# Attention and a Mish layer on one core: a new order for the head of the kernel, and the last tile in two banks

## The chip, the cores and the metric

The kernel runs on one core of a Trainium2 chip. The metric is device time in microseconds (us) of one execution. A core has a matrix engine (TensorE, PE in the profile; PEld is its weight load), VectorE (DVE), ScalarE (ACT), GpSimd (POOL) and SyncE (SP), which work side by side, each through its own instructions in order. They meet through semaphores. Matrix results go to PSUM, eight banks of 128 x 512 fp32; everything else is in SBUF. DMAs are issued here from SP's queue and from ACT's.

## What is computed

x is 2048 x 512 in bf16. It is normalised once, and two branches read the result and are added to x.

```python
xn = layernorm(x)                                   # over 512, eps 1e-5
# A: linear attention, 32 heads of 16
q, k, v = xn @ wqkv                                 # 512 -> 3 x 512
pq, pk  = q @ w_phi, k @ w_phi                      # 16 x 16 for each head
phi     = concat(softmax(p), softmax(-p))           # for q and for k
kv, z   = phi_k^T v, sum over rows of phi_k         # 32 x 16 for each head
o       = (phi_q kv) / (phi_q z + 1e-6)
# B: a layer with Mish
act     = mish(xn @ w1 + b1)                        # 512 -> 1792
out     = x + o @ wo + act @ w2
```

## The kernel before, in words

The 2048 rows are 16 tiles of 128, four to a group. The order of all instructions is written out by hand: each engine executes what the program text gives it, in that order (`manual_schedule`), and only semaphores and the reuse of buffers make it wait.

w_phi is multiplied into the weights first. `fold` (L93) takes a transposed weight `wT` (512 x 512, read by a DMA transposition on SP, L90) and the block-diagonal `Wbd` (made by DVE at L458), and writes `wkp` for the keys, later `wqp` for the queries. Then `logits(s, i, copy)` (L188) is four matmuls of 128 x 512 and a copy into `p_sb`; s = 0 to 3 are the keys of the four groups, s = 4 to 7 the queries. `value` (L160) is the same with `wv`, copied into `vext`. `hidden(n)` (L168) does n units of the Mish layer, each four matmuls and one Mish on ACT; there are 56 units, 14 to a group.

For a softmax of p and of -p, `extremes(s)` (L194, DVE) subtracts the maximum and the minimum of each 16 columns, `exponentials(s)` (L223, ACT) takes two activations of 128 x 2048, and `normalise(s, k)` (L240, DVE) sums, inverts and multiplies. `accumulate(g)` (L274) adds phi_k^T v into `pkv`, which has three PSUM banks; `mask_kv` (L288) takes it out. For the queries, `attend(h, i)` (L312) multiplies with kv into `pnd` (the same three banks) and four ACT copies take that out; `combine(h)` (L341, DVE) divides and has the result turned by a DMA. `second_layer(t)` (L388) is 14 matmuls for tile t, `project_out(h)` (L397) adds o @ wo for two tiles in the same bank, and `residual` (L409, DVE) adds x and sends the rows out.

**PSUM.** Five banks (`ps`, tag mm) go round among folds, turns, logits, values, hidden units and second-layer tiles: the sixth user waits until the first user's bank has been read. Three banks (`ps2`, tag kv) hold pkv, then pnd; before, they are pkv's from the start, zeroed by DVE at L439.

**The head.** SP issues x's tiles 0 and 1 (L415), the transposition of the keys' weight (L418), then the rest of x, wv, w1. ACT's queue issues w_phi, x's tiles 2 and 3, and b1. Twelve matmuls on the identity (L450) warm PE. `ln_stats` (L110) makes mean and variance of tiles on DVE, and POOL makes the reciprocal root by an add and a power (L119, L122); `ln_apply` (L125) is one DVE instruction for each tile. Tiles 0 to 3 are turned by PE (`ln_turn_pe`, L136), later ones by DMA (`ln_turn_dma`, L144). Then follow fold, logits of group 0, `extremes(0)` with the normalisation of group 1 inside, four values and four hidden units.

**The loop** (L496) has, for s = 0 to 3: exponentials(s), accumulate(s - 1), two values copied by DVE, logits(s + 1), two values copied by ACT, statistics of a later group, normalise(s), hidden units (16, 14, 8, 10), extremes(s + 1). So on ACT the copies of logits(s + 1) come after exponentials(s), and on DVE the value copies come after extremes(s). After the loop come accumulate(3), logits(5), second_layer(0), two hidden units, attend(0, 0), two more, attend(0, 1), second_layer(1), and then a pipeline over eight pairs of tiles (L543). At its end tile 15 has its four matmuls of o @ wo in two halves of 256 columns in one bank, so that the first half can leave while the second is made; DVE reads the bank between them.

## Time and profile before

| | |
|---|---|
| median of 3 runs | 186.38 us (186.23 to 186.47) |
| profiled execution | 186.27 us |
| its span, first to last instruction | 184.5 us |
| mean granted clock of TensorE | 0.996 |
| busy: PE, DVE, ACT, POOL | 175.5, 149.4, 126.8, 8.2 us |
| first real matmul | 6.74 us |
| end of PE's last matmul | 181.4 us |

Times in the views are us from the start of the span. A timeline line has start, duration, engine, line, operation, what it writes <- what it reads, shape, and in brackets the engine's idle time ahead of it with what ended it; like instructions in a row are merged (x4), and the duration then spans all of them. A line of the waits has engine, instruction and line, what it waited for, and the total, the number of times and the longest wait in us. Ends of matmuls are modelled: a matmul of 128 x 512 is shown as 379 ns, but the next one starts 216 ns after it.

### The profile page before, as it was taken

What the parts mean: (1) busy time and instruction counts of PE and PEld (TensorE: products, weight loads), DVE (VectorE), ACT (ScalarE), POOL (GpSimd) and SP (SyncE); (2) the same over time, 40 slices, a digit from 0 to 9 for tenths busy, and PEclk for the clock granted to TensorE, in tenths of its full rate; (3) what the DMA queues carried; (4) which work ended last, traced back from release to release, by engine and by line L of the source; (5) the groups of instructions that cost most, each with busy time, mean ns of one, the idle gap of its engine ahead of it and who ended that gap; (6) DMA issues with size and microseconds to landing.
All of it is one profiled execution on the core that took longest, in us unless ns stands there. A gap on an engine that the chain in (4) does not pass through costs nothing.

```text
span 184.5 us, 2715 instructions
## 1 busy us (share of the span) xinstructions
PE 175.5 (95%) x1011; PEld 89.0 (48%) x1025; DVE 149.4 (81%) x263; ACT 126.8 (69%) x196; POOL 8.2 (4%) x22
## 2 busy tenths in 40 slices
PE   6799879999999999999999999999999999999991
PEld 2454334464444645644464555555554545455440
DVE  4989999987999989989999784299916996738962
ACT  2357999989888799969986999272842567244200
POOL 4403020000200000000000000000000000000000
PEclk9999999999999999999999999999999999999998
DMA  5997899000091000000000922943079302990732
GB/s 144 298 407 240 175 361 205 0 0 5 6 187 35 4 0 0 0 0 4 0 0 1 191 39 56 187 101 60 0 171 207 77 5 58 199 197 2 89 111 88
DMA packets 44394, 18.02 MB, mean 98 GB/s; under 512 B 36829, under 2 KB 43869, under 8 KB 44381
## 3 DMA queue, kind: packets, MB, share of 16 engines
q1 hardware_dynamic: 43408, 17.50, 39.9%
q10 hardware_dynamic: 972, 0.35, 0.7%
q8 instruction: 8, 0.13, 0.3%
q14 instruction: 6, 0.04, 0.1%
HBM read 6.84 MB, written 2.10 MB: 48 GB/s over the span
## 4 chain that ended last, share of the span: by engine, by line
PE 87%; ACT 5%; DVE 3%; DMA 2%; issue 1%
PE po L392 26%; PE ph L174 24%; PE pproj L154 21%; PE po L403 7%; PE pnd L323 4%; PE pkv L279 4%; ACT e L226 2%; DMA x_sb<-in_A_x_dram 2%; DVE stats L116 1%; ACT acts L181 1%; DVE x_sb L411 1%; ACT L181 1%; ACT L226 0%; PE pfold L98 0%; PE ptr L139 0%
## 5 line engine op out<-in xcount | busy, mean ns | idle before, releaser
L174 PE MATMUL ph<-xnT,w_sb 128*128 128x512 bf16 x224 | 49.7, 379 | 1.2 <-ACT p_sb L192 1.2
L392 PE MATMUL po<-w_sb,acts 128*128 128x512 bf16 x218 | 50.0, 379 | 0.3
L181 ACT ACTIVATE acts<-ph,b1f 128x512 bf16<-128x512 f32 x56 | 35.4, 695 | 3.5 <-PE ph L174 3.2
L174 PEld LDWEIGHTS <-w_sb 128*128 128x128 bf16 x224 | 21.8, 98 | 27.3 <-issue 1.5
L226 ACT ACTIVATE e<-e 128x2048 bf16<-128x2048 bf16 x16 | 29.7, 1902 | 7.2 <-DVE e L216 7.2
L392 PEld LDWEIGHTS <-acts 128*128 128x128 bf16 x224 | 21.5, 98 | 23.3
L154 PEld LDWEIGHTS <-xnT 128*128 128x128 bf16 x192 | 18.3, 97 | 22.6 <-DMA xnT<-xn 1.2
L192 ACT CAST p_sb<-pproj 128x512 bf16<-128x512 f32 x29 | 15.7, 585 | 9.0 <-PE pproj L154 9.0
L411 DVE TENSOR_TENSOR x_sb<-po,x_sb 128x512 bf16<-128x512 f32 (+1 forms) x17 | 10.7, 655 | 13.3 <-PE po L403 13.3
L244 DVE TENSOR_REDUCE s<-e 128x128 f32<-128x2048 bf16 x8 | 18.2, 2279 | 1.6 <-ACT e L226 1.6
L403 PE MATMUL po<-wqk,ob 128*128 128x512 bf16 (+1 forms) x66 | 14.7, 366 | 0.7 <-DVE x_sb L411 0.7
L154 PE MATMUL pproj<-wkp,xnT 128*128 128x512 bf16 x62 | 14.5, 379 | 0.9 <-DMA xnT<-xn 0.8
L154 PE MATMUL pproj<-wv,xnT 128*128 128x512 bf16 x61 | 15.0, 379 | 0.2
L154 PE MATMUL pproj<-wqk,xnT 128*128 128x512 bf16 x63 | 14.4, 379 | 0.1
L332 ACT CAST wkp<-pnd 128x768 bf16<-128x768 f32 x8 | 6.4, 804 | 10.5 <-PE pnd L323 6.5
L205 DVE TENSOR_TENSOR m<-m 128x512 bf16<-128x512 bf16 (+1 forms) x32 | 11.5, 359 | 1.1
L205 DVE TENSOR_TENSOR m<-p_sb 128x1024 bf16<-128x1024 bf16 x16 | 11.0, 685 | 1.0 <-ACT p_sb L192 1.0
L332 ACT CAST wv<-pnd 128x768 bf16<-128x768 f32 x8 | 6.3, 793 | 7.3 <-PE pnd L323 5.1
L323 PEld LDWEIGHTS <-qT 128*128 128x128 bf16 x128 | 9.1, 98 | 3.8
L116 DVE BATCH_NORM_STATS2 stats<-x_sb 128x6 f32<-128x512 bf16 x16 | 9.9, 679 | 1.2 <-DMA x_sb<-in_A_x_dram 1.2
L323 PE MATMUL pnd<-kvm,qT 128*128 128x144 bf16 x128 | 10.6, 226 | 0.1
L403 PEld LDWEIGHTS <-ob 128*128 128x128 bf16 x68 | 6.6, 98 | 7.7 <-issue 0.9
(64 smaller groups left out, 171.2 us busy)
## 6 DMA issues: line engine op xcount, KB each, us to landing
w_sb<-in_B_w_dram SPq DMA_DIRECT2D x2, 1792.0 KB, 8.7
out_dram<-x_sb SPq DMA_DIRECT2D x15, 128.0 KB, 1.8
x_sb<-in_A_x_dram SPq DMA_DIRECT2D x1, 1024.0 KB, 11.2
x_sb<-in_A_x_dram SPq DMA_DIRECT2D x1, 512.0 KB, 4.0
wv<-in_A_wqkv_dram SPq DMA_DIRECT2D x1, 512.0 KB, 4.9
wqk<-in_A_wo_dram SPq DMA_DIRECT2D x1, 512.0 KB
x_sb<-in_A_x_dram SPq DMA_DIRECT2D x1, 256.0 KB, 3.2
x_sb<-in_A_x_dram ACTq DMA_DIRECT2D x1, 256.0 KB, 3.5
```

The costliest lines, as they stand in the source:

```text
L154: nc.tensor.matmul(pp[:], lhsT=xnT[:, t, kt, :], rhs=w[:, kt, :], start=(kt == 0), stop=(kt == KT - 1),)
L174: nc.tensor.matmul(ph[:], lhsT=w1_sb[:, kt, f * P : (f + 1) * P], rhs=xnT[:, g * TPG : (g + 1) * TPG, kt, :], start=(kt == 0), stop=(kt == ...
L181: nc.scalar.activation(acts[:, f, g * 512 : (g + 1) * 512], ph[:], ACT.Mish, bias=b1f[:, f : f + 1])
L192: copy(p_of[s][:, i, :], pp[:])
L205: nc.vector.tensor_tensor(out=m[:], in0=src[:, :, 0:half], in1=src[:, :, half : 2 * half], op=op)
L226: nc.scalar.activation(v, v, ACT.Exp)
L244: nc.vector.reduce_sum(t[:], v.rearrange("p t l (c e) -> p (t l c) e", e=16), axis=AX.X)
L323: nc.tensor.matmul(blocks(pnd, pl, j, 144), lhsT=qT_of[h][:, i, pl * 4 + j, :], rhs=kvm[:, pl, j, :], start=True, stop=True,)
L332: nc.scalar.copy(to[:, :, 0:3, :], a)
L392: nc.tensor.matmul(po[:], lhsT=acts[:, f, t * P : (t + 1) * P], rhs=w2_sb[:, f, :], start=(f == 0), stop=(t == NT - 1 and f == FT - 1),)
L403: nc.tensor.matmul(po[:, c], lhsT=oT_of[h][:, i * 4 + j, :], rhs=wo_sb[:, j, c], start=False, stop=(j == 3 or len(cuts) == 2), skip_group_ ...
L411: nc.vector.tensor_tensor(out=y, in0=po[:, c], in1=y, op=ALU.add)
```

## The change

- ACT's queue issues x's tiles 0 and 1 first, then w_phi, tiles 2 and 3, and wv; SP issues the weight's transposition first, then tiles 4 to 7, b1, w1 and the rest.
- For tiles 0 to 3, the reciprocal root is a Sqrt on ACT (with an eps tile as bias) and a reciprocal on DVE. One Sqrt on eps comes early, behind ACT's DMA issues. Statistics, roots and applications go tile by tile for tiles 0 and 1.
- POOL makes eps first, and takes over the three casts for the masks from DVE. Nine warm-up matmuls instead of twelve.
- PE turns tile 0 before the fold; three of the fold's four blocks go to kv's banks. value(0) comes behind the fold and the turn of tile 1, ahead of the logits.
- Six hidden units instead of four ahead of exponentials(0). In s = 0, the first tile of logits(1) has an ordinary bank and is copied between the two exponentials; the other three go to kv's banks, and one ACT copy of 128 x 1536 takes them out after six further hidden units.
- pkv takes kv's banks after that copy; DVE zeroes it there, between normalise(0, 1) and extremes(1).
- Hidden units: 6, then 6 + 11, 14, 8, 9 and 2, where there were 4, then 16, 14, 8, 10 and 2 + 2. The first eight matmuls of second_layer(1) stand where the last two units stood.
- Tile 15 has two banks: its second layer is made in halves of 256 columns, and so is its o @ wo.

```diff
--- before.py
+++ after.py
@@ -75,6 +75,8 @@
     wqp = wqk[:, :, 0:D]
     wo_sb = wqk[:, :, D : 2 * D]
     ident = consts.tile([P, P], BF16, name="ident")
+    eps = consts.tile([P, 1], FP32, name="eps")
+    root = consts.tile([P, 1], FP32, name="root")
     mhalf = consts.tile([P, TPG], FP32, name="mhalf")
     block = consts.tile([P, 8, 16], BF16, name="block")
     KVmask = consts.tile([P, 136], FP32, name="KVmask")
@@ -90,10 +92,13 @@
         nc.sync.dma_start_transpose(out=wT[:], in_=A_wqkv[:, base_col : base_col + D])
         return wT
 
-    def fold(wT, dst, dve):
+    def fold(wT, dst, dve, banks=None):
 
         for kt in range(KT):
-            pf = ps.tile([P, 512], FP32, name="pfold", tag="mm")
+            if banks is not None and kt < 3:
+                pf = banks[:, kt, :]
+            else:
+                pf = ps.tile([P, 512], FP32, name="pfold", tag="mm")[:]
             for j in range(4):
                 nc.tensor.matmul(
                     pf[:, j * P : (j + 1) * P],
@@ -103,9 +108,9 @@
                     stop=True,
                 )
             if kt in dve:
-                nc.vector.tensor_copy(dst[:, kt, :], pf[:])
+                nc.vector.tensor_copy(dst[:, kt, :], pf)
             else:
-                nc.scalar.copy(dst[:, kt, :], pf[:])
+                nc.scalar.copy(dst[:, kt, :], pf)
 
     def ln_stats(t0, n):
 
@@ -147,12 +152,13 @@
             in_=xn[:, i : i + 2, :].rearrange("p t c -> p (t c)"),
         )
 
-    def project(w, t):
-
-        pp = ps.tile([P, 512], FP32, name="pproj", tag="mm")
+    def project(w, t, pp=None):
+
+        if pp is None:
+            pp = ps.tile([P, 512], FP32, name="pproj", tag="mm")[:]
         for kt in range(KT):
             nc.tensor.matmul(
-                pp[:], lhsT=xnT[:, t, kt, :], rhs=w[:, kt, :],
+                pp, lhsT=xnT[:, t, kt, :], rhs=w[:, kt, :],
                 start=(kt == 0), stop=(kt == KT - 1),
             )
         return pp
@@ -160,7 +166,7 @@
     def value(t, copy):
         pv = project(wv, t)
         copy(
-            vext[(t // TPG) % 2][:, t % TPG, :, 0:128], pv[:].rearrange("p (j c) -> p j c", j=4)
+            vext[(t // TPG) % 2][:, t % TPG, :, 0:128], pv.rearrange("p (j c) -> p j c", j=4)
         )
 
     units = iter([(g, f) for g in range(NG) for f in range(FT)])
@@ -189,7 +195,7 @@
         if i == 0:
             p_of[s] = smx.tile([P, TPG, 512], BF16, name="p_sb", bufs=1)
         pp = project(wkp if s < NG else wqp, (s % NG) * TPG + i)
-        copy(p_of[s][:, i, :], pp[:])
+        copy(p_of[s][:, i, :], pp)
 
     def extremes(s, between=None):
 
@@ -220,8 +226,8 @@
                 op=ALU.subtract,
             )
 
-    def exponentials(s):
-        for k in range(2):
+    def exponentials(s, ks=(0, 1)):
+        for k in ks:
             v = e_of[s][:, 2 * k : 2 * k + 2, :, :]
             nc.scalar.activation(v, v, ACT.Exp)
             if s >= NG:
@@ -268,10 +274,10 @@
         v = kv[:, :, 0:432].rearrange("p b (k c) -> p b k c", c=144)
         return v[:, 0:2, :, c0:c1], v[:, 2, 0:2, c0:c1]
 
-
-    pkv = ps2.tile([P, 3, 512], FP32, name="pkv", tag="kv")
+    kv_of = {}
 
     def accumulate(g):
+        pkv = kv_of[0]
         e = e_of.pop(g)
         for j in range(4):
             for pl in range(2):
@@ -286,7 +292,7 @@
                     )
 
     def mask_kv():
-
+        pkv = kv_of[0]
 
         a, b = by_parts(pkv, 0, 136)
         nc.vector.tensor_tensor(
@@ -385,26 +391,28 @@
                 in_=o_t[:, q].rearrange("p i c -> p (i c)"),
             )
 
-    def second_layer(t):
-        po = ps.tile([P, 512], FP32, name="po", tag="mm")
-        po_of[t] = po
-        for f in range(FT):
-            nc.tensor.matmul(
-                po[:], lhsT=acts[:, f, t * P : (t + 1) * P], rhs=w2_sb[:, f, :],
-                start=(f == 0), stop=(t == NT - 1 and f == FT - 1),
-            )
+    def halves(t):
+        return (slice(0, 256), slice(256, 512)) if t == NT - 1 else (slice(0, 512),)
+
+    def second_layer(t, f0=0, f1=FT):
+        if f0 == 0:
+            po_of[t] = [ps.tile([P, 512], FP32, name="po", tag="mm") for _ in halves(t)]
+        for po, c in zip(po_of[t], halves(t)):
+            for f in range(f0, f1):
+                nc.tensor.matmul(
+                    po[:, c], lhsT=acts[:, f, t * P : (t + 1) * P], rhs=w2_sb[:, f, c],
+                    start=(f == 0), stop=False,
+                )
 
     def project_out(h):
-        for i in range(2):
-            po = po_of.pop(2 * h + i)
-            cuts = (slice(0, 256), slice(256, 512)) if (h, i) == (7, 1) else (slice(0, 512),)
-            for n, c in enumerate(cuts):
+        for t in (2 * h, 2 * h + 1):
+            for po, c in zip(po_of.pop(t), halves(t)):
                 for j in range(4):
                     nc.tensor.matmul(
-                        po[:, c], lhsT=oT_of[h][:, i * 4 + j, :], rhs=wo_sb[:, j, c],
-                        start=False, stop=(j == 3 or len(cuts) == 2), skip_group_check=len(cuts) == 2,
+                        po[:, c], lhsT=oT_of[h][:, t % 2 * 4 + j, :], rhs=wo_sb[:, j, c],
+                        start=False, stop=(j == 3),
                     )
-                residual(2 * h + i, po, c, nc.sync if n or len(cuts) == 1 else nc.scalar)
+                residual(t, po, c, nc.scalar if c.stop == 256 else nc.sync)
 
     def residual(t, po, c, queue):
         y = x_sb[:, t, c]
@@ -412,14 +420,16 @@
         queue.dma_start(o_v[:, t, c], y)
 
 
-    nc.sync.dma_start(x_sb[:, 0:2, :], x_v[:, 0:2, :])
+    nc.gpsimd.memset(eps[:], 1e-5)
+    wT = load_turned(D)
+    nc.scalar.dma_start(x_sb[:, 0:2, :], x_v[:, 0:2, :])
     with nc.allow_non_contiguous_dma(reason="tiny w_phi load"):
         nc.scalar.dma_start(wsrc[:], wphi_v)
-    wT = load_turned(D)
     nc.scalar.dma_start(x_sb[:, 2:4, :], x_v[:, 2:4, :])
-    nc.scalar.dma_start(b1b[:], b1_v[:, :])
+    nc.scalar.dma_start(wv[:], wqkv_v[:, :, 2 * D : 3 * D])
+    nc.scalar.activation(root[:], eps[:], ACT.Sqrt)
     nc.sync.dma_start(x_sb[:, 4:8, :], x_v[:, 4:8, :])
-    nc.sync.dma_start(wv[:], wqkv_v[:, :, 2 * D : 3 * D])
+    nc.sync.dma_start(b1b[:], b1_v[:, :])
     nc.sync.dma_start(w1_sb[:], w1_v[:, :, :])
     nc.sync.dma_start(x_sb[:, 8:16, :], x_v[:, 8:16, :])
 
@@ -436,10 +446,9 @@
     nc.gpsimd.memset(mhalf[:], -0.5)
     for i in range(2):
         nc.gpsimd.memset(vext[i][:, :, :, 128:136], 1.0)
-    nc.vector.memset(pkv[:, :, 0:432], 0.0)
-    nc.vector.tensor_copy(KVmask[:, 0:P], block[:].rearrange("p h d -> p (h d)"))
-    nc.vector.tensor_copy(KVmask[:, P : P + 8], block[:, :, 0])
-    nc.vector.tensor_copy(
+    nc.gpsimd.tensor_copy(KVmask[:, 0:P], block[:].rearrange("p h d -> p (h d)"))
+    nc.gpsimd.tensor_copy(KVmask[:, P : P + 8], block[:, :, 0])
+    nc.gpsimd.tensor_copy(
         kvm[:].rearrange("p l j c -> p (l j) c")[:, :, 136:144],
         block[:, None, :, 0].to_broadcast([P, 8, 8]),
     )
@@ -448,33 +457,57 @@
     dve, act = nc.vector.tensor_copy, nc.scalar.copy
 
     warm = ps.tile([P, 4, P], FP32, name="warm", tag="mm")
-    for _ in range(12):
+    for _ in range(9):
         nc.tensor.matmul(
             warm[:], lhsT=ident[:], rhs=ident[:, None, :].to_broadcast([P, 4, P]),
             start=True, stop=True,
         )
 
-    st0 = ln_stats(0, 2)
+    xn = lnp.tile([P, TPG, D], BF16, name="xn", tag="xn")
+    hstats = lnp.tile([P, TPG, nc.vector.BN_STATS_DIM], FP32, name="hstats", bufs=1)
+    hmv = lnp.tile([P, TPG, nc.vector.BN_AGGR_DIM], FP32, name="hmv", bufs=1)
+    hrstd = lnp.tile([P, TPG], FP32, name="hrstd", bufs=1)
+
+    def spread(t):
+        nc.vector.bn_stats(hstats[:, t, :], x_sb[:, t, :])
+
+    def root_of(t, n):
+        for i in range(t, t + n):
+            nc.vector.bn_aggr(hmv[:, i, :], hstats[:, i, :])
+        nc.scalar.activation(hrstd[:, t : t + n], hmv[:, t : t + n, 1], ACT.Sqrt, bias=eps[:])
+
+    def apply(t, n):
+        nc.vector.reciprocal(hrstd[:, t : t + n], hrstd[:, t : t + n])
+        ln_apply(t, n, hmv[:, t : t + n, :], hrstd[:, t : t + n], xn, t)
+
+    spread(0)
+    root_of(0, 1)
+    spread(1)
+    apply(0, 1)
     nc.vector.tensor_tensor(
         out=Wbd[:].rearrange("p j (h e) -> p j h e", h=8),
         in0=block[:, None, :, :].to_broadcast([P, 4, 8, 16]),
         in1=wsrc[:, :, None, :].to_broadcast([P, 4, 8, 16]),
         op=ALU.mult,
     )
-    st1 = ln_stats(2, 2)
-    xn = lnp.tile([P, TPG, D], BF16, name="xn", tag="xn")
-    ln_apply(0, 2, *st0, xn, 0)
-    fold(wT, wkp, (3,))
-    ln_turn_pe(0, xn, 0, dve)
+    root_of(1, 1)
+    spread(2)
+    apply(1, 1)
+    ln_turn_pe(0, xn, 0, act)
+    fold(wT, wkp, (3,), ps2.tile([P, 3, 512], FP32, name="pfolds", tag="kv"))
     ln_turn_pe(1, xn, 1, act)
+    spread(3)
+    root_of(2, 2)
+    value(0, act)
+    for i in range(2):
+        logits(0, i, act)
+    apply(2, 2)
+    ln_turn_pe(2, xn, 2, dve)
+    ln_turn_pe(3, xn, 3, act)
     pb = ps.tile([P, 512], BF16, name="pb", tag="mm")
     nc.tensor.transpose(pb[:, 0:FT], b1b[:], ident[0:FT, 0:FT])
-    ln_apply(2, 2, *st1, xn, 2)
-    logits(0, 0, act)
+    nc.vector.tensor_copy(b1f[:], pb[:, 0:FT])
     for i in range(2, 4):
-        ln_turn_pe(i, xn, i, dve)
-    nc.vector.tensor_copy(b1f[:], pb[:, 0:FT])
-    for i in range(1, TPG):
         logits(0, i, act)
 
     def normal(t0, st, xn):
@@ -487,21 +520,27 @@
     extremes(0, lambda: normal(TPG, st, xn))
     nc.sync.dma_start(w2_sb[:], w2_v[:, :, :])
     nc.sync.dma_start(wo_sb, wo_v[:, :, :])
-    for i in range(TPG):
+    for i in range(1, TPG):
         value(i, act)
-    hidden(4)
-
-
+    hidden(6)
 
     for s in range(NG):
-        exponentials(s)
+        exponentials(s, (0, 1) if s else (0,))
         if s > 0:
             accumulate(s - 1)
         if s < NG:
             for i in range(2 if s else 0):
                 value(s * TPG + i, dve)
-        for i in range(TPG):
-            logits(s + 1, i, act)
+        if s == 0:
+            p_of[1] = smx.tile([P, TPG, 512], BF16, name="p_sb", bufs=1)
+            act(p_of[1][:, 0, :], project(wkp, TPG))
+            exponentials(0, (1,))
+            wide = ps2.tile([P, 3, 512], FP32, name="pwide", tag="kv")
+            for i in range(3):
+                project(wkp, TPG + 1 + i, wide[:, i, :])
+        else:
+            for i in range(TPG):
+                logits(s + 1, i, act)
         if 0 < s < NG:
             for i in range(2, TPG):
                 value(s * TPG + i, act)
@@ -517,7 +556,12 @@
         normalise(s, 1)
         if s == 2:
             fold(wT, wqp, ())
-        hidden((16, 14, 8, 10, 4)[s])
+        if s == 0:
+            hidden(6)
+            act(p_of[1][:, 1:4, :], wide[:])
+            kv_of[0] = ps2.tile([P, 3, 512], FP32, name="pkv", tag="kv")
+            nc.vector.memset(kv_of[0][:, :, 0:432], 0.0)
+        hidden((11, 14, 8, 9)[s])
         extremes(s + 1)
 
 
@@ -529,10 +573,10 @@
     second_layer(0)
     hidden(2)
     attend(0, 0)
-    hidden(2)
+    second_layer(1, 0, 8)
     attend(0, 1)
     extremes(5)
-    second_layer(1)
+    second_layer(1, 8)
     combine(0)
     exponentials(5)
     second_layer(2)
```

## The prediction, made before the changed kernel was seen to run

> **What bounds the kernel.** I read the busy line first, then who TensorE (PE) waited for, then the chain that ended last, then the timeline of each engine where the waits fall.
>
> ```profile
> PE 175.5 (95%) x1011; PEld 89.0 (48%) x1025; DVE 149.4 (81%) x263; ACT 126.8 (69%) x196; POOL 8.2 (4%) x22
> ```
>
> PE is busy for 175.5 of 184.5 us, and the chain is 87% PE. The change neither removes nor adds PE work (only three warm-up matmuls, which lie before the first real one), so what can be won is idle time of PE. The list of PE's waits holds all of it, but for the output's way out after the last matmul:
>
> ```profile
> PE warm L452 <- POOL ident masks.py:199: 1.4, 1, 1.4
> PE ph L174 <- ACT p_sb L192: 1.2, 1, 1.2
> PE pproj L154 <- DMA xnT<-xn: 0.8, 1, 0.8
> PE po L403 <- DVE x_sb L411: 0.7, 1, 0.7
> PE ptr L139 <- DVE wkp L106: 0.6, 1, 0.6
> PE pfold L98 <- DMA wT<-in_A_wqkv_dram: 0.5, 1, 0.5
> ```
>
> The real work starts with the fold at 6.74. What I call a group below is four matmuls of 128x512: 0.216 us each (32 in 6.91 in the chain), 0.865 together. The 1.2 and 0.8 us are one place: ScalarE (ACT) is filled from 17 to 28 us, and L192's copies, which free the banks of the logits, stand behind the exponentials:
>
> ```profile
> 17.19 1.28 ACT L181 ACT_TABLE_LOAD   x1
> 18.48 2.42 ACT L181 ACTIVATE acts<-ph,b1f 128x512 bf16<-128x512 f32 x4
> 20.92 1.28 ACT L226 ACT_TABLE_LOAD   x1
> 22.21 3.71 ACT L226 ACTIVATE e<-e 128x2048 bf16<-128x2048 bf16 x2
> 25.83 2.03 ACT L192 CAST p_sb<-pproj 128x512 bf16<-128x512 f32 x4
> ```
>
> From 26.45 to 177 PE waits for nobody longer than 0.05 us. Whatever time is won before that is kept only as far as VectorE (DVE) and ACT keep up.
>
> **The head.** Before, x's first pair of tiles lands at 4.00 (issued 0.79 on SP). Now it goes out on ACT's queue beside wT's transposition. The nearest row is x's second pair, which went out on ACT at 1.29 beside the same transposition and took 3.5: I take 0.78 + 3.5 = 4.28, with 4.00 as the early end. The issues on ACT (0.46, 0.48, 0.56 and 0.51 by their rows) end at 2.9, the table load (1.28) at 4.2, so the warm-up root is out of the way. wT's issue moves from 1.31 to 0.79; it took 5.4 to land, so 6.2; undisturbed (the second wT, 4.4) 5.2; with all of wv (512 KB at the 284 GB/s of that stretch, 1.8 us) ahead of its last part 8.0. I take 6.2, since beside x it has been measured.
>
> DVE then: statistics of tile 0 to 4.95 (0.68), aggregation to 5.1, root on ACT to 5.45 (no such row: 0.22 for a 128x32 copy, plus the 0.11 by which a Mish with a bias exceeds a copy of its size), reciprocal about 0.16 (0.553 for 64 columns, 0.352 for 32, extended to one) behind tile 1's statistics to 5.9, apply to 6.3, Wbd (0.39) to 6.65. PE turns tile 0 at 6.35 and folds from 6.75 to 7.65, which is when it folds now: wT stops being late, and Wbd is what is late next. ACT goes through tile 1's root (7.1), xnT's copy (7.68) and three fold copies at 0.5 to 9.15. PE turns tile 1 (8.0), fills the gap with value(0) (8.4 to 9.25, wv landing by about 8 by the bytes ahead of it), and runs logits 0 and 1 to 11.0. Tiles 2 and 3: DVE's fold copy (8.65), statistics (9.3), aggregations (9.6), root, reciprocal and applies (10.95); turned by 11.45, xnT copied by 11.8, logits 2 and 3 to 13.55, three values to 16.15. Before, the same work ended at 16.38. **The head wins 0.2 us.** POOL's three casts for the masks, the memset of eps and DVE's relief before 4 us are worth nothing: DVE idled there until x came, and the masks are read at 98 us. SP's remaining loads go out up to 0.5 earlier or with b1b (0.71) between; w1 landed by 14.6 and is read at 16.15.
>
> **The ACT knot.** Six hidden groups now go ahead of the exponentials: 16.15 + 6 x 0.865 = 21.34. From there ACT's order is: the last Mish (0.17 after the matmul, 0.69) to 22.2, table 1.3 to 23.5, exponential 1.9 to 25.4, one copy 0.5 to 25.9, exponential to 27.8, table to 29.1, Mish to 29.75: 8.4 us until the bank that hidden group 11 needs is free. PE has four logits (one in an ordinary bank, three in kv's) and hidden groups 6 to 10 to do meanwhile, 9 x 0.865 = 7.8. So 0.6 us of idle remain where 1.95 were. The logits' xnT comes at 21.75 (DVE reaches the extremes 1.0 later than at 13.75, and PE got its tile at 20.75); that 0.4 lies inside the 0.6. Then hidden 11 to 22 take 10.4: accumulate(0) starts at 40.15. Before it started at 39.56 with 20 hidden groups done instead of 23: 3 x 0.865 - 0.59 = **2.0 us won here**. The wide copy (1.44 by extension from 0.80 for 768 columns) ends at 34.2; hidden 17 needs the Mish behind it at 34.8 and gets it at 34.9, nothing worth counting.
>
> **What comes back.** DVE gets a 1.14 us memset of pkv, and its reduction waits for the first exponential (25.4 instead of 24.1). Before, DVE ran without a hole from 24.16 to the end of extremes(1) at 40.92 and then waited 1.45 for PE. Now it ends at 25.4 + 16.76 + 1.17 = 43.35; with the two value copies (1.37) behind it, the next statistics begin at 44.72 instead of 43.83, 0.9 late, while PE is 0.6 late. In s=1 and s=2 the banks still come 0.4 us before they are needed. In s=3 there is no slack today: the last value waits for the first logits copy, 0.04 us.
>
> ```profile
> 84.87 1.56 ACT L192 CAST p_sb<-pproj 128x512 bf16<-128x512 f32 x3
> 85.02 1.02 PE L154 MATMUL pproj<-wv,xnT 128*128 128x512 bf16 x4
> ```
>
> The extremes, exponentials and sums there form a chain, 0.9 late, so PE loses 0.3. One hidden group fewer in s=3 brings accumulate(3) to 94.7, as before. After it, eight matmuls of second_layer(1) stand where two hidden groups stood (equal, 1.73, but without two Mishes), yet ACT is 0.9 late: logits copy 103.4, table, two Mishes, the four copies out of pnd to 107.3; attend(0,1) waits from 107.0, 0.35 lost. After that attend(1,1) waits for copies that end at 115.7 and project_out(0) for a transposition that lands at 116.3, against 117.62 before: 1.3 us are kept. From there DVE and ACT had waits of 1 to 5 us on PE, and move along.
>
> **The tail.**
>
> ```profile
> 179.72 1.02 DVE L411 TENSOR_TENSOR x_sb<-po,x_sb 128x512 bf16<-128x512 f32 x2 [0.17 <-PE po L403]
> 180.80 0.60 PE L403 MATMUL po<-wqk,ob 128*128 128x256 bf16 x4 [0.68 <-DVE x_sb L411]
> 181.43 0.42 DVE L411 TENSOR_TENSOR x_sb<-po,x_sb 128x256 bf16<-128x256 f32 x1 [0.69 <-PE po L403]
> ```
>
> With the halves in two banks PE does not wait for DVE, and the last sum follows the one before at 180.75: it ends at 181.17 instead of 181.85. The 28 half matmuls cost what 14 whole ones do, some 0.03 more. The fifth bank was freed by a residual that ended at 174.1, needed at 175.4. **0.65 us won.**
>
> Sum: 2.0 - 0.3 - 0.35 - 0.05 + 0.65 = 2.0 (rounded). The profiled execution took 186.27 (span 184.5 and 1.8 around it), 0.1 under the median 186.38: **184.3 us**.
>
> **Two rules.** Warm-up: the matmuls of L452 started 0.43 apart until about 5.3, 3.9 us after the first, and the fold's then 0.055 apart, so the array began at half speed, though the granted clock of those rows reads 1.00. Nine now end at about 5.3. The Trainium skill ("TensorE: Matmul & The Clock Gate", Part 1) says that full speed takes a busy window of about 3.4 us, free-running, and that the moment varies; it speaks against taking three away, and by it the gate could still be shut. Table switches: a copy ended at 17.16 and the Mish behind the load began at 18.48, 1.3 in all. The skill ("ScalarE: Activation LUTs", What ACT_TABLE_LOAD costs) puts 2.66 with a drain; by it the knot above would grow by 2.7. The trace shows no drain, and the sum goes by it. Copies at 25.83 came without a load after Exp, so the root's table takes the place of the first load and adds none.
>
> **Rivals.** (1) The head comes late by 1.1 to 1.6 and PE with it. Either wT lands at 8.0: fold to 8.9, its copies to 10.0, logits 1.1 later; or the array is still at half speed from 6.35 until 3.9 us of dense work after 8.4: fold 0.9, value and logits 0.9 each, less 1.1 of waits that absorb it, 1.6. For it: the head's margin for wT is 0.5; against: the rows beside x. 185.4 to 185.9. (2) The give-backs do not happen (exponentials a little earlier, x at 4.00): 2.0 + 0.65 + 0.3 = 2.95, 183.3. For it: each is under 0.4 us and hangs on one slack. (3) Slower: x's first pair, now on another queue, is served after wT instead of before it. All of the head hangs on it one for one. Price: its landing past 4.28; no change at 6.3 (wT's own landing), slower by over 0.2% from about 6.7. Against it: the 3.5 us of the second pair beside wT. (4) It does nothing: the knot's idle returns at s=1 to 3, because DVE is later than 0.9. From 45.4 as the end of extremes(1), 2.0 more, all is gone; the three us of slack before extremes(1) reads the wide copy speak against it.
>
> **Chances.** Forecast (183.6 to 185.1) 0.58; (1) 0.18; (2) 0.12; (3) 0.06; (4) and whatever else cancels 0.06. Range 183.2 to 185.7, which leaves out the slow edge of (1), (3), (4) and a corner of (2). The measurement tells about 0.2%, 0.4 us: faster 0.87, same 0.07, slower 0.06.
>
> **What the profile after would show.** Fold at 6.7 to 6.9, waiting for Wbd, not for wT; hidden from 16.2; PE idle 0.6 around 21 to 30; extremes(1) ending near 43.4; a wait of the last value of s=3 near 85.9; no DVE wait ahead of the last four matmuls. A fold whose matmuls start 0.11 apart, or statistics after 5 us, would make the forecast wrong.

## The result and the profile after

The changed kernel takes **187.28 us** (median of 22 runs, 185.8 to 189.44) where the kernel before takes 186.31 (22 runs, 186.1 to 186.68): ratio 1.0055, 95% interval 1.0038 to 1.0071. It is slower, where the forecast was 184.3. Here and below the interval is made of each kernel's shorter executions alone, the median of all of them, so for a kernel whose executions spread, as this one's do, the two need not agree. The profiled execution took 188.75 (span 187.0 and 1.75 around it), one of the longer ones; before, 186.27.

Read the busy line and the list of TensorE's (PE's) waits first, as before. The busy line of the changed kernel:

```profile
PE 178.2 (95%) x1021; PEld 91.6 (49%) x1036; DVE 148.6 (79%) x261; ACT 128.0 (68%) x200; POOL 6.8 (4%) x22
```

PE is busy 2.7 us longer with no more work to do, so some matmuls ran slower. Its waits (engine and line, what for: us in total, times, longest):

```profile
PE pfolds L103 <- ACT wkp L113: 1.5, 2, 0.8
...
PE ph L180 <- ACT acts L187: 0.4, 1, 0.4
PE pproj L160 <- DMA wv<-in_A_wqkv_dram: 0.3, 1, 0.3
PE pfolds L103 <- DVE Wbd L487: 0.3, 1, 0.3
```

The knot's wait (L192, 1.2), the transposition's (0.8) and the last residual's (0.7) are gone; 0.4 is left where 0.6 was forecast. On top stands a wait that I had not written down: the fold's matmuls for the fold's own copies. PE's timeline from the fold on (start, length, what, how many; in brackets the idle time before and its releaser):

```profile
5.70 0.61 PE L144 MATMUL ptr<-ident,xn 128*128 128x128 bf16 x4 [0.23 <-DVE xn L132]
6.56 0.58 PE L103 MATMUL pfolds<-Wbd,wT 128*128 128x128 bf16 x4 [0.26 <-DVE Wbd L487]
7.94 0.58 PE L103 MATMUL pfolds<-Wbd,wT 128*128 128x128 bf16 x4 [0.80 <-ACT wkp L113]
9.20 0.59 PE L103 MATMUL pfolds<-Wbd,wT 128*128 128x128 bf16 x4 [0.67 <-ACT wkp L113]
...
10.01 0.63 PE L144 MATMUL ptr<-ident,xn 128*128 128x128 bf16 x4
10.98 1.87 PE L160 MATMUL pproj<-wv,xnT 128*128 128x512 bf16 x4 [0.35 <-DMA wv<-in_A_wqkv_dram]
12.64 2.68 PE L160 MATMUL pproj<-wkp,xnT 128*128 128x512 bf16 x8
...
20.39 1.89 PE L180 MATMUL ph<-xnT,w_sb 128*128 128x512 bf16 x8
```

and before, the fold, the first hidden groups and the first accumulation:

```profile
6.74 1.07 PE L98 MATMUL pfold<-Wbd,wT 128*128 128x128 bf16 x16 [0.54 <-DMA wT<-in_A_wqkv_dram]
...
16.38 3.62 PE L174 MATMUL ph<-xnT,w_sb 128*128 128x512 bf16 x16
...
39.40 2.06 PE L279 MATMUL pkv<-vext,e 128*128 128x136 bf16 x32
```

The fold starts at 6.56, close to the 6.75 that was forecast, but takes until 10.0 instead of 7.65. Value(0) starts at 10.98 (forecast 8.4) and takes 1.87, where four such matmuls took 1.02 in the kernel before, at 85.02; the eight of the logits take 2.68 where eight take 1.89 at 20.39. Already tile 0's turning (four matmuls at 5.70) takes 0.61, where the same takes 0.40 at full speed (h0_held below), so in this execution the array was at half speed from the start until about 14. The hidden groups start at 20.39: forecast 16.15, before 16.38. **The head is 4.0 us later than before.** That is one of the longer executions; if the parts behind the head are the same in all, the median of 187.28 means a head later by about 2.5 (an estimate: 0.97, what the medians differ by, + 1.6 for the knot - 0.1, from below).

Two other engines' timelines say what else is late. SyncE's (SP's) issues, before:

```profile
1.31 3.39 SPq L90 DMA_TRANSPOSE wT<-in_A_wqkv_dram  x1
4.76 0.57 SPq L421 DMA_DIRECT2D x_sb<-in_A_x_dram  x1
```

and after:

```profile
0.79 1.38 SPq L92 DMA_TRANSPOSE wT<-in_A_wqkv_dram  x1
2.22 1.33 SPq L431 DMA_DIRECT2D x_sb<-in_A_x_dram  x1
3.61 0.52 SPq L432 DMA_DIRECT2D b1b<-in_B_b_dram  x1
4.17 0.40 SPq L433 DMA_DIRECT2D w_sb<-in_B_w_dram  x1
```

and VectorE's (DVE's) after:

```profile
3.64 0.69 DVE L472 BATCH_NORM_STATS2 hstats<-x_sb 128x6 f32<-128x512 bf16 x1 [3.64 <-DMA x_sb<-in_A_x_dram]
...
8.09 0.69 DVE L472 BATCH_NORM_STATS2 hstats<-x_sb 128x6 f32<-128x512 bf16 x1 [1.49 <-DMA x_sb<-in_A_x_dram]
8.70 0.14 DVE L480 RECIPROCAL hrstd<-hrstd 128x1 f32<-128x1 f32 x1
```

x's first pair came early (3.64; forecast 4.28). But the transposition's issue held SP 1.38 us instead of 3.39, so x's tiles 4 to 7 (512 KB) went out 2.5 us sooner than before, and w1 1.75 sooner. They share the DMA engines with what ScalarE's (ACT's) queue brings: x's second pair lands at 8.0, and wv at 10.9, 8.6 us after its issue. Tile 1's reciprocal (8.70) stands on DVE behind tile 2's statistics, so tile 1 could not be turned before 9.3.

Behind the head all is as forecast. The one line for the array's next big step:

```profile
44.38 2.06 PE L285 MATMUL pkv<-vext,e 128*128 128x136 bf16 x32
```

From the start of the hidden groups it is 44.38 - 20.39 = 23.99 (forecast 24.0). From there to the end of the span it is 187.0 - 44.38 = 142.6; before, it was 184.5 - 39.40 = 145.1 with three more hidden groups still to do (2.59), so 142.5 for the same work. So give-backs and tail cancel within 0.1, as forecast (0.7 against 0.65). The residuals of the tail run without a hole:

```profile
183.02 1.35 DVE L419 TENSOR_TENSOR x_sb<-po,x_sb 128x512 bf16<-128x512 f32 x3 [0.17 <-PE po L411]
```

### The profile page after: what moved, and what is told of

It is laid out like the page before. It is cut to its first block, busy times and chain, and to the rows that moved or that the text cites. A ratio compares the mean times of both kernels' runs of the same rounds, so it can differ in the third digit from the quotient of the medians.

```text
span 187.0 us, 2740 instructions
## 1 busy us (share of the span) xinstructions
PE 178.2 (95%) x1021; PEld 91.6 (49%) x1036; DVE 148.6 (79%) x261; ACT 128.0 (68%) x200; POOL 6.8 (4%) x22
## 4 chain that ended last, share of the span: by engine, by line
DVE 42%; PE 36%; ACT 11%; DMA 6%; issue 3%; ACTq 1%; DVEq 0%
PE po L402 19%; DVE m L211 9%; DVE e L222 7%; DVE s L250 7%; PE po L411 7%; PE pproj L160 6%; ACT e L232 6%; DMA wv<-in_A_wqkv_dram 5%; DVE e L263 4%; DVE stats L121 4%; PE pnd L329 3%; ACT acts L187 3%; DVE r L258 3%; DVE m L217 2%; DMA ob<-ob 2%
## 5 line engine op out<-in xcount | busy, mean ns | idle before, releaser
L402 PE MATMUL po<-w_sb,acts 128*128 128x512 bf16 (+1 forms) x232 | 50.4, 366 | 0.3
L187 ACT ACTIVATE acts<-ph,b1f 128x512 bf16<-128x512 f32 x56 | 34.8, 702 | 2.2 <-PE ph L180 1.9
L402 PEld LDWEIGHTS <-acts 128*128 128x128 bf16 x238 | 22.8, 98 | 22.0
L160 PEld LDWEIGHTS <-xnT 128*128 128x128 bf16 x192 | 18.9, 100 | 23.6 <-issue 3.1
L198 ACT CAST p_sb<-pproj 128x512 bf16<-128x512 f32 x25 | 13.7, 587 | 9.9 <-PE pproj L160 9.9
L419 DVE TENSOR_TENSOR x_sb<-po,x_sb 128x512 bf16<-128x512 f32 (+1 forms) x17 | 10.6, 654 | 11.3 <-PE po L411 11.3
L160 PE MATMUL pproj<-wv,xnT 128*128 128x512 bf16 x61 | 16.0, 395 | 0.6 <-DMA wv<-in_A_wqkv_dram 0.3
L160 PE MATMUL pproj<-wkp,xnT 128*128 128x512 bf16 x51 | 12.8, 398 | 0.2 <-DVE xnT L147 0.2
L211 DVE TENSOR_TENSOR m<-p_sb 128x1024 bf16<-128x1024 bf16 x16 | 10.9, 682 | 1.0 <-ACT p_sb L198 1.0
L329 PE MATMUL pnd<-kvm,qT 128*128 128x144 bf16 x128 | 10.6, 226 | 0.2 <-ACT ds L345 0.2
L222 DVE TENSOR_TENSOR e<-p_sb,m 128x2048 bf16<-128x2048 bf16 x8 | 9.8, 1226 | 0.3
L222 DVE TENSOR_TENSOR e<-m,p_sb 128x2048 bf16<-128x2048 bf16 x8 | 9.8, 1226 | 0.3
```

The costliest lines, as they stand in the source:

```text
L160: nc.tensor.matmul(pp, lhsT=xnT[:, t, kt, :], rhs=w[:, kt, :], start=(kt == 0), stop=(kt == KT - 1),)
L187: nc.scalar.activation(acts[:, f, g * 512 : (g + 1) * 512], ph[:], ACT.Mish, bias=b1f[:, f : f + 1])
L198: copy(p_of[s][:, i, :], pp)
L211: nc.vector.tensor_tensor(out=m[:], in0=src[:, :, 0:half], in1=src[:, :, half : 2 * half], op=op)
L222: nc.vector.tensor_tensor(out=e[:, :, pl, :].rearrange("p t (c e o) -> p t c e o", e=8, o=2), in0=p5 if pl == 0 else mb, in1=mb if pl == 0 ...
L329: nc.tensor.matmul(blocks(pnd, pl, j, 144), lhsT=qT_of[h][:, i, pl * 4 + j, :], rhs=kvm[:, pl, j, :], start=True, stop=True,)
```

## The experiments

Theory A: the fold's three pieces lie in one tile (kv's three banks), and each piece's matmuls wait for the copy of the one before. Theory B: SP's later loads, issued sooner, take the DMA engines from x's second pair and wv. Theory C: with three warm-ups fewer the array stays at half speed until 14. Rival: the head is a side show, and the knot or the tail lost it.

In all these kernels every transposing DMA is replaced by a plain DMA of the same bytes, so nothing is transposed: wk is folded, and the rest computed, on untransposed data. They are compared among themselves.

```diff
-nc.sync.dma_start_transpose(out=wT[:], in_=A_wqkv[:, base_col : base_col + D])
+nc.sync.dma_start(wT[:], wqkv_v[:, :, base_col : base_col + D])
```

(and the other three alike). **The two stand-ins**: b0_plain is the kernel before, a0_plain the changed one.

> The kernel before with every DMA transposition (of the weights, of xn, of the exponentials and of o) replaced by a plain DMA of the same bytes, so nothing is transposed there; all else is left. It is the base for the runs that follow. Both theories: the transposed weight lands earlier (no 1.4 to 3.4 us of issue), so the fold starts up to 1 us earlier than 6.74, and the transpositions in the knot land about 1 us earlier; the rest of the kernel is bound by PE as before: 185.0 to 186.3.

> The changed kernel with every DMA transposition replaced by a plain DMA of the same bytes, so nothing is transposed there. Theory A (the fold's matmuls wait for the copy of the block before, because three blocks lie in one tile) and theory B (x's second pair and wv are late because SP's later loads share the DMA engines): both work without transpositions too, so this is slower than or equal to the kernel before with plain DMAs, 186.0 to 187.5, with waits of 0.6 to 0.8 us at the fold and wv landing past 9 us. Rival D (the transposition itself, beside ordinary loads, is what delays them): the loads land by about 6 and 8 us and the time falls to 184.5 to 185.5.

b0_plain: 187.72 (186.6 to 188.82), ratio to before 1.0061 [1.0034, 1.0089]. a0_plain: 194.01 (193.45 to 194.72), 1.0407 [1.0386, 1.0427]. A plain weight's issue takes 0.44, so SP's loads go out sooner still (tiles 4 to 7 at 1.29, w1 at 2.40), and ACT's queue fares worse: wv takes 13.9 us to land, against 8.6 in the changed kernel and 4.9 before (there on SP's queue; 7.2 in b0_plain), and the hidden groups start at 26.7. That is B, exaggerated.

**From a0_plain, A undone alone, then B alone.** The fold's matmuls all first, then its copies:

```diff
+        made = []
         for kt in range(KT):
...
+            made.append(pf)
...
+        for kt, pf in enumerate(made):
             if kt in dve:
```

> The changed kernel with plain DMAs in place of the transpositions (nothing is transposed there), and the fold makes the matmuls of all four blocks first and copies afterwards (kv's banks kept). Theory A: the waits at the fold disappear and the fold ends about 1.5 us earlier; if wv lands late (theory B) value(0) then waits for it, and only 0 to 0.5 us are gained over the changed kernel with plain DMAs; if wv is early, 1.0 to 1.5. Without theory A: the same waits and the same time.

194.2 (193.69 to 194.7), 1.0418 [1.04, 1.0435]: the fold's waits are gone, and nothing is won, since wv still takes 13.6. Now x's second pair and wv on SP, ahead of tiles 4 to 7:

```diff
-    nc.scalar.dma_start(x_sb[:, 2:4, :], x_v[:, 2:4, :])
-    nc.scalar.dma_start(wv[:], wqkv_v[:, :, 2 * D : 3 * D])
+    nc.sync.dma_start(x_sb[:, 2:4, :], x_v[:, 2:4, :])
+    nc.sync.dma_start(wv[:], wqkv_v[:, :, 2 * D : 3 * D])
     nc.sync.dma_start(x_sb[:, 4:8, :], x_v[:, 4:8, :])
```

> The changed kernel with plain DMAs in place of the transpositions (nothing is transposed there), and x's second pair and wv are issued on SP behind the weight and ahead of tiles 4 to 7, not on ACT's queue. Theory B: x's second pair lands by about 5.5 and wv by about 8; tile 1 is normalised up to 2 us earlier; 0.5 to 1.0 us gained over the changed kernel with plain DMAs, and less spread. If B is wrong they land as late as before and the time is the same.

188.87 (188.02 to 189.68), 1.0132 [1.0108, 1.0156]: 5.1 us off, with wv landing 6.4 after its issue. The fold still waits 1.7.

**Loads held.** To take B out of both sides, SP's loads from tiles 4 to 7 on wait for x's second pair, through a one-element write by GpSimd (which the load then overwrites). hb_held is b0_plain so, h0_held a0_plain; h1 is h0 with the fold first, h2 is h1 with twelve warm-ups. (In a0_plain and the held kernels made from it x's first pair, issued beside the plain weight, lands at 5.5 to 5.9, where it came at 3.64 in the changed kernel; so their heads start later.)

```diff
+    nc.gpsimd.tensor_copy(x_sb[:, 4, 0:1], x_sb[:, 2, 0:1])
     nc.sync.dma_start(x_sb[:, 4:8, :], x_v[:, 4:8, :])
```

> The kernel before with plain DMAs in place of the transpositions (nothing is transposed there), and SP's loads from tiles 4 to 7 on held back until x's second pair has landed. Theory B (loads issued early on SP take the DMA engines from the ones that the head waits for): x's second pair lands near 5 instead of 6.5 and the time falls by 0.5 to 1.0 from 187.7. Otherwise the same 187.7. It is the base for the next three.

> The changed kernel with plain DMAs in place of the transpositions (nothing is transposed there), and SP's loads from tiles 4 to 7 on held back until x's second pair has landed. Theory B: w_phi lands near 4.5 instead of 9 to 10, x's second pair near 5.5 instead of 13, wv near 7 instead of 16, and the time falls from 194.0 to 186.0 to 187.0, where theory A's waits at the fold (1.5 us) and theory C's half-speed matmuls remain. If the loads are late for another reason (ACT's queue itself), they stay late and the time above 190.

> As the run before (plain DMAs, SP's loads held), and the fold makes all matmuls first and copies afterwards. Theory A: now that the loads are early the fold's waits show: 0.8 to 1.5 us less than the run before. Without theory A, or if value(0) waits for wv all the same: within 0.3.

> As the run before (plain DMAs, SP's loads held, fold's matmuls first), with twelve warm-up matmuls. Theory C: the fold's matmuls start 0.055 apart and value(0)'s 0.216 in the profile, and 0.5 to 1.0 us are gained; the hidden units begin near 16.2, the forecast's own figure, and the time is 184.3 to 185.0. If the gate opens late in either, within 0.3 of the run before.

| kernel | us, median (range) | ratio to before |
|---|---|---|
| hb_held | 186.76 (186.56 to 187.03) | 1.0017 [1.0009, 1.0026] |
| h0_held | 188.5 (187.89 to 189.46) | 1.0115 [1.009, 1.014] |
| h1_held_fold | 186.49 (185.16 to 186.65) | 0.9994 [0.9979, 1.0008] |
| h2_held_fold_warm | 185.51 (185.05 to 186.49) | 0.9951 [0.9935, 0.9968] |

B is shown for the stand-ins: with the loads held, wv, still on ACT's queue, lands 5.8 after its issue instead of 13.9, and 5.5 us come off a0_plain. With B out, A is worth 2.0, and the warm-ups 1.0 more. PE's timeline of h0_held shows why A is worth more than its 1.7 of waits:

```profile
7.55 0.40 PE L144 MATMUL ptr<-ident,xn 128*128 128x128 bf16 x4 [2.09 <-DVE xn L132]
7.88 0.38 PE L103 MATMUL pfolds<-Wbd,wT 128*128 128x128 bf16 x4
9.26 0.59 PE L103 MATMUL pfolds<-Wbd,wT 128*128 128x128 bf16 x4 [0.99 <-ACT wkp L113]
...
11.75 1.91 PE L160 MATMUL pproj<-wv,xnT 128*128 128x512 bf16 x4
```

The first piece takes 0.38, full speed; after a wait of 0.99 the second takes 0.59, and value(0) 1.91. Between them (and after the 2.1 that PE waited ahead of tile 0's turning) the array falls back to half speed. The spread of b0_plain, too, goes with half speed: its six executions of 186.6 to 187.0 have a mean granted clock of 0.996 to 1.0, its six of 188.45 to 188.82 one of 0.986 to 0.991. In its profiled execution the fall does not lie in the head but in the knot, from 27.4 to 30.8, behind a wait of 2.07 us; in hb_held PE waits 0.78 and 1.00 there and does not fall.

**Behind the head** (rival: it lost there). From hb_held, the tail in two banks alone; everything behind the head but the tail; both, which is the whole change without its head:

> The kernel before with plain DMAs in place of the transpositions (nothing is transposed there) and SP's loads held, and of the change only the last tile in two banks. The forecast's tail: PE no longer waits 0.7 us for the sum on VectorE ahead of its last four matmuls; 0.5 to 0.65 us less than the same kernel without it (186.8), so 186.1 to 186.3. Rival: the end is set by the DMA of the last rows, or the 28 half matmuls cost more than 14 whole ones: within 0.2 of 186.8.

> The kernel before with plain DMAs in place of the transpositions (nothing is transposed there) and SP's loads held, with the head of before (x first, roots on GpSimd, fold in ordinary banks, four values after the logits), and of the change the part after it: six hidden units ahead of the exponentials, three logits in kv's banks with one wide copy, pkv zeroed later, the new counts of hidden units, second_layer(1) begun early. The forecast's knot: 24.0 us from the end of the values to accumulate(0), 1.4 to 1.8 us less idle time on PE, of which 0.6 come back in s=3 and at attend(0,1): 0.7 to 1.2 less than 186.8, so 185.6 to 186.1. Rival: VectorE's later memset and sums give back all of it: 186.6 to 186.9.

> As the run before, with the last tile in two banks as well: everything of the change but its head. If the head alone made the changed kernel slower, this gains both parts: 1.2 to 1.8 us less than 186.8, so 185.0 to 185.6, and it beats the kernel before. Rival (the rest of the change loses too): 186.4 or more.

k1_tail 186.02 (185.82 to 186.56), 0.74 under hb_held; ratio to before 0.9985 [0.9976, 0.9994]. k2_knot 185.86 (185.42 to 186.42), 0.90 under; 0.9976 [0.9966, 0.9986]. k3_knot_tail **185.23** (184.69 to 185.32), 1.53 under; 0.9936 [0.9923, 0.9949]. (By the ratios, each against the kernel before as measured beside it, they are 0.6, 0.8 and 1.5 under hb_held.) The two parts add up, and the rival falls: all that lies behind the head wins.

**Realistic timing.** g0_timed_base is a0_plain with SP's issues put off by GpSimd writes to about the times of the changed kernel (weight 1.47, tiles 4 to 7 at 2.68, w1 at 4.00; there 0.79, 2.22, 4.17). Then one theory is undone at a time: gA_fold_first has the fold's matmuls first (as above), gB_loads_held holds tiles 4 to 7 for x's second pair and w1 for wv, gC_warm12 has twelve warm-ups, gABC_all has all three:

```diff
+        nc.gpsimd.memset(wT[:, 0, 0:1], 0.0)
...
+    nc.gpsimd.tensor_copy(x_sb[:, 4, 0:1], block[:, 0, 0:1])
...
+    nc.gpsimd.tensor_copy(w1_sb[:, 0, 0:1], x_sb[:, 0, 0:1])
...
-    for _ in range(9):
+    for _ in range(12):
```

(the last two lines in gC_warm12 and gABC_all only)

> The changed kernel with plain DMAs in place of the transpositions (nothing is transposed there), with small writes on GpSimd that set the issues near where the changed kernel has them: the weight at about 1.5 us, tiles 4 to 7 and b1 from 2.4, w1 and the rest once x's first pair has landed (about 4). All theories: x's first pair near 3.7, w_phi 4 to 6, x's second pair 6 to 8, wv 9 to 11, and 186.7 to 188.0, like the changed kernel's 187.3. If it is above 189, the base is still worse than the changed kernel.

> The same (plain DMAs, timed issues) with all of the fold's matmuls ahead of its copies. Theory A alone decides: 1.0 to 1.5 us less than the timed base. If the loads decide (B): at most 0.4 less, because value(0) waits for wv and tile 1 for x.

> The timed base (plain DMAs), but tiles 4 to 7 and b1 held until x's second pair has landed, and w1 and the rest until wv has. Theory B alone decides: 1.0 us or more less than the timed base; if the fold's serial matmuls and copies decide (A): at most 0.4 less, since value(0) comes behind the fold.

> The timed base (plain DMAs) with twelve warm-up matmuls. Theory C as first put (three matmuls too few): 0.7 to 1.5 us less. If the gate shuts because PE idles between the short pieces of the head, whatever the warm-up was: within 0.4.

> g0_timed_base with all three undone: fold matmuls first and then the copies, SP's loads held as in gB_loads_held, twelve warm-ups. If the head's three faults are what cost, and add to one another, it is below each alone: 184.5 to 185.2. If the serial fold is the only one of weight, it stands with gA_fold_first, 185.3 to 185.8. If the clock gate falls as it likes, the median is above 186 and the executions spread.

| kernel | us, median (range) | ratio to before |
|---|---|---|
| g0_timed_base | 188.3 (185.09 to 189.85) | 0.9989 [0.9955, 1.0024] |
| gA_fold_first | 185.52 (184.6 to 187.6) | 0.9962 [0.9936, 0.9989] |
| gB_loads_held | 187.71 (185.06 to 189.32) | 1.0013 [0.9979, 1.0047] |
| gC_warm12 | 186.12 (185.0 to 189.19) | 0.9987 [0.9952, 1.0021] |
| gABC_all | 185.75 (185.13 to 186.72) | 0.9973 [0.9956, 0.9989] |

g0_timed_base, gB and gC spread over 4 to 5 us, and the intervals of g0, gA, gB and gC overlap, so the ratios settle no difference among them. Undoing A takes 2.8 off the median, B 0.6, C 2.2. What these medians count is shown by the granted clock of each execution, and by the trace of a longer one, gC_warm12:

```profile
7.39 0.38 PE L105 MATMUL pfolds<-Wbd,wT 128*128 128x128 bf16 x4 [0.49 <-DMA wT<-in_A_wqkv_dram]
8.45 0.38 PE L105 MATMUL pfolds<-Wbd,wT 128*128 128x128 bf16 x4 [0.67 <-ACT wkp L115]
9.51 0.38 PE L105 MATMUL pfolds<-Wbd,wT 128*128 128x128 bf16 x4 [0.67 <-ACT wkp L115]
9.73 0.48 PE L105 MATMUL pfold<-Wbd,wT 128*128 128x128 bf16 x4
...
10.43 1.91 PE L162 MATMUL pproj<-wv,xnT 128*128 128x512 bf16 x4
```

With twelve the fold runs at full speed, and then the array drops to half all the same, before value(0). The row of the granted clock (one digit for a fortieth of the span, in tenths) shows the drop in its third place, 9.3 to 14.0:

```profile
PEclk9969999999999999999999999999999999999999
```

The row of the changed kernel shows nothing:

```profile
PEclk9999999999999999999999999999999999999999
```

The mean granted clock of this gC_warm12 execution is 0.991, so (1 - 0.991) x 186.0 x 2 = 3.3 us went at half speed. All five of its executions from 187.7 to 189.2 have a mean of 0.982 to 0.991, and the seven from 185.0 to 186.3 have 0.997 to 1.0: the two groups are executions with and without such a drop. Half speed that lasts from the start, as in the changed kernel's profile, is not counted; so a mean of 1.0 in a long execution (188.0 to 188.4 in g0) does not speak against it.

By mean clock and time together, the array seems to have kept full speed in one of ten executions of g0 (185.1), two of twelve of gB (185.1 and 185.2), eight of twelve of gA (184.6 to 185.9), seven of twelve of gC (185.0 to 186.3) and all twelve of gABC (185.1 to 186.7). These times lie close together in all five kernels. So most of what the medians differ by is how often the array keeps full speed; the fold's waits as such cost little here, which rests on the single such execution of g0, and it was not profiled.

gA_fold_first, with nine, does not drop in its profiled execution:

```profile
5.97 0.83 PE L107 MATMUL pfolds<-Wbd,wT 128*128 128x128 bf16 x12
...
9.46 1.02 PE L165 MATMUL pproj<-wv,xnT 128*128 128x512 bf16 x4 [1.31 <-ACT hrstd L485]
```

Theory C is not confirmed as I put it, since twelve do not keep the array at full speed by themselves, but the count does matter. In the profiled executions with the new head, tile 0's turning takes 0.61 in five of nine with nine warm-ups (the changed kernel, a0, a1, h1, g0) and 0.39 or 0.40 in all five with twelve. From h1 to h2 the executions with a mean clock of 0.991 go from eight of eleven to one of eight. (That one is the profiled one of h2: full speed was reached in the warm-up and lost again as the fold began, whose first twelve matmuls take 1.42, where they take 0.83 in gA_fold_first.) So the thin fold (4 matmuls, a wait, 4 matmuls) costs its waits where nothing else is late, and it makes it likelier that the array is at half speed behind it. All three undone (gABC_all) makes the executions agree within 1.6 us, but is no faster than A alone: in its trace the hold let w1 go so late that the first hidden group waited 1.36 for it.

**A better head.** k4 is h2_held_fold_warm with x's first pair on SP ahead of the weight, as before the change; k5 is k4 with the loads held for x's first pair only:

```diff
-    nc.scalar.dma_start(x_sb[:, 0:2, :], x_v[:, 0:2, :])
+    nc.sync.dma_start(x_sb[:, 0:2, :], x_v[:, 0:2, :])
     wT = load_turned(D)
...
-    nc.gpsimd.tensor_copy(x_sb[:, 4, 0:1], x_sb[:, 2, 0:1])
+    nc.gpsimd.tensor_copy(x_sb[:, 4, 0:1], x_sb[:, 0, 0:1])
```

> The changed kernel with plain DMAs in place of the transpositions (nothing is transposed there), SP's loads held, fold's matmuls first and twelve warm-up matmuls (185.5 so far), and x's first pair issued on SP ahead of the weight, as before. If the weight ahead of x is what makes x's first pair land at 5.5 instead of 3.7, this starts the head 1.5 us earlier; the fold then waits for the weight (landing 6.5) instead: 0.5 to 1.0 us less, so 184.5 to 185.0. If the transposed weight sets the head in both orders, within 0.3 of 185.5.

> k4_new_head_x_first (184.89), with SP's loads from tiles 4 to 7 on held until x's first pair has landed, and no longer until the second. There the first hidden group waited 1.29 us for w1, the values having ended by 15.7. If that wait is all that the hold costs, 183.6 to 184.2. If the loads, let go 2 us sooner, take the share of the DMA engines from the second pair and wv, tile 2 and the values come late and it stays at 184.9 or goes above.

k4: 184.89 (184.02 to 185.5), ratio 0.9922 [0.9899, 0.9946], with 1.3 of waiting for w1. k5: **184.06** (four executions, 183.96 to 184.10), 0.9876 [0.9862, 0.9889], 2.18 below the kernel before as measured beside it (186.24), and below hb_held by 2.70 (1.4% by the two ratios). PE's timeline of k5_w1_sooner is the one that I forecast (fold 6.75, value(0) 8.4, hidden 16.15, accumulate 40.15):

```profile
6.82 0.84 PE L105 MATMUL pfolds<-Wbd,wT 128*128 128x128 bf16 x12
...
8.25 1.02 PE L163 MATMUL pproj<-wv,xnT 128*128 128x512 bf16 x4
...
16.07 5.34 PE L183 MATMUL ph<-xnT,w_sb 128*128 128x512 bf16 x24
...
40.06 2.06 PE L288 MATMUL pkv<-vext,e 128*128 128x136 bf16 x32
```

k5 is not a finished kernel: it transposes nothing, and the same head with transposing DMAs was not tried.

## Why the prediction was wrong

**The step that failed is the head**: "PE turns tile 0 at 6.35 and folds from 6.75 to 7.65", and behind it "value(0) (8.4 to 9.25 ...)" and "The head wins 0.2 us". It lost 4.0 in the profiled execution. The sign that I had named, fold matmuls that start 0.11 apart, was there. Three things stood in place of the win.

- *The fold.* I let PE run 16 matmuls in a row and ACT copy behind it. The diff puts the first three pieces into slices of one tile, and there each piece waits for the copy of the one before (0.80 and 0.67). Before, each piece had a tile of its own, and all 16 ran in a row, in 1.07. My wait list named what the fold needs, not what its output waits for.
- *The loads.* "SP's remaining loads go out up to 0.5 earlier": it was 2.5 and 1.75. I moved the issue of the transposition with its old length (3.39). Nor did I charge it for the bytes: wv "landing by about 8" came at 10.9, x's second pair at 8.0. A share of this would have been seen by asking what the queue behind the moved issue then sends.
- *The array's speed.* The sum had full speed from the fold on; half speed stood only in rival 1, until 3.9 us of dense work after 8.4, at 1.6. It lasted to about 14 and cost 0.85 in value(0) and 0.8 in the first logits, besides the fold. What the prediction quoted against taking three warm-ups away was so in this execution.

By the trace, the hidden groups start 4.24 later than forecast. Of these, 2.58 lie ahead of value(0) (10.98 against 8.4) and 1.58 between it and the turning of tile 2 (15.16 - 10.98 against 11.0 - 8.4), where PE never waits and only the half speed is different; 0.1 lies behind. Ahead of value(0) the fold and the loads lie side by side in the changed kernel: the fold ends at 10.0, tile 1 could be turned at 9.3, and wv lands at 10.9, so by this trace undoing one alone would leave value(0) near 10.6 to 10.9, as I estimate (a1_fold_first, with still later loads, won nothing). How the 2.58 divide is argued, not shown, because all experiments replaced the transposition.

The spread of 3.6 us goes with the array's speed here as well. Of the 22 executions only the shortest, 185.8, joins a mean granted clock of 1.0 to a short time; 15 have 0.991 (186.6 to 187.9), two 0.979 and 0.982 (189.3 and 189.4), and four long ones read 1.0 (188.3 to 188.8), the profiled one with its half speed from the start among them. Even 185.8 is 1.5 above the forecast, so the half speed is not the whole loss. What decides which execution keeps full speed stays open.

**Right were the steps behind the head.** The knot took 23.99 (24.0). Its win was mis-sized: before, the accumulation starts at 39.40 by the timeline, not 39.56 (about where the merged line of hidden matmuls ends, and such ends are modelled), so the knot alone wins 39.40 - 16.38 + 2.59 - 23.99 = 1.6; the forecast's 2.0 held those 0.16 and the 0.2 of the head. Give-backs and tail cancel as forecast; the tail measured alone is 0.6 to 0.74 (0.65). The three stretches add up to what the profiled executions differ by, as they must: 4.0 - 1.6 + 0.1 = 2.5 (188.75 - 186.27 = 2.48).

**Rivals.** (1) had the half speed and priced it at 1.6, near the 1.58 that the trace shows from value(0) on; but it stood alone there, so 185.9 was too low. (3), x's first pair behind the weight, did not happen: 3.64 (in a0_plain and h0_held, with the plain weight, it did: 5.87 and 5.50). (2) and (4) were not put to the test in the changed kernel, as the head hid them; k3_knot_tail, 1.5 under hb_held, speaks against (4). No rival held the chain inside the fold, the output of a step waiting in its own tile.

**The pages.** The Trainium skill ("Trainium Kernel Development and Optimization", Key Constraints) says that DMAs issued by several engines run on the same 16 DMA engines and interleave, so that another queue saves issue time only. The runs agree: issued on ACT's queue, wv lands 5.8 us after its issue where SP's later loads are held (h0_held), 8.6 in the changed kernel, and 13.9 where SP sends sooner still (a0_plain); in the kernel before, on SP's queue ahead of w1, it took 4.9. The same skill ("TensorE: Matmul & The Clock Gate", HAM oscillation) gives idle gaps above about 3.4 us as the danger, and behind that (A second HAM failure mode: psum-queue depth-cycling) a kernel whose short idles between groups of matmuls re-throttled it. Here pieces of 0.38 us with waits of 0.5 to 0.7 went ahead of the drop (gC_warm12): this trace is nearer to the second case.

## What to carry to other kernels

When a group of results is put into slices of one tile to save banks, put all their matmuls ahead of the first copy, or give each a tile; one that writes and reads the same tile in turn runs as a chain. When a slow issue moves or shortens, list what its queue sends next and whose transfers it will meet; "earlier" is a cost for the others. Look at the array's speed by the length of equal matmuls, not once at the start but after every stretch in which it works in short pieces; and when executions of one kernel spread, put their mean granted clocks beside their times.

## What the runs showed of the hardware

- The issue of one and the same transposition took SP 3.39 us behind a load of x and 1.38 as the first of its queue.
- The array fell back to half speed while it worked in short pieces with waits of 0.5 to 0.7 us (gC_warm12: matmuls of 0.38 for four, then 1.91 for value(0)).
- The granted clock shows such a fall (0.5 in gC_warm12 between about 9.9 and 13.3) but not a half speed that lasts from the start: it reads 1.0 for the whole execution of the changed kernel, where tile 0's turning takes 0.61 and value(0) 1.87.
- Loads held back made executions agree: b0_plain spread over 2.2 us, hb_held over 0.5; the longer executions of b0_plain are those with a mean granted clock of 0.991 or less.
